# GpSimd takes the clamp of the weights' conversion, and TensorE transposes the identity in its early gaps

## The chip, the cores and the metric

The kernel runs on one core of a Trainium2 chip. The metric is device microseconds (us) of one execution, as the median of several. The core's engines are named as in the profile: PE (TensorE, matrix products and transposes), DVE (VectorE), ACT (ScalarE), POOL (GpSimd) and SP (SyncE, which only issues loads and stores here).

## The reference

What is computed, cut to its core (batch 8, 8 heads, 576 positions, head dimension 64; 4608 tokens, model width 512, inner width 2048):

```python
q_s = np.exp(q - np.max(q, axis=-1, keepdims=True))
q_s = q_s / (np.sum(q_s, axis=-1, keepdims=True) + 1e-09)
k_s = np.exp(k - np.max(k, axis=2, keepdims=True))
k_s = k_s / (np.sum(k_s, axis=2, keepdims=True) + 1e-09)
kv = np.einsum('bhsd,bhse->bhde', k_s, v)
attn = np.einsum('bhsd,bhde->bhse', q_s, kv)        # x: its rows by token, 4608 x 512
r = np.maximum(x @ w_in, 0.0)
out = (s * (r * r) + b) @ w_out
```

Inputs and outputs reach the kernel as float32; the weights arrive in HBM as 64-bit numbers, two 32-bit words each.

## The kernel before

**Work.** Tokens go in 9 blocks of 512 (one for each batch element, 512 of its 576 positions, and a last one of the 64 left over from each). A block has 16 steps, one for each 128 columns of the inner width. Step t makes `h` (12 products of 128x512, line 693), r = relu(h), s r² + b split into a high part `gh` and a low part `gl` (lines 718 to 737), and adds 12 products into the accumulator `acc` (line 760). Every operand is split into two float32r parts, high and low, so three products stand for one. The 144 steps make up nearly all of PE's time.

**Attention.** A head pair u (two heads, four of them in a batch element) gives 128 rows of x. In block 0 and 1 keys and queries are worked on by `k_stream`, `k_pair`, `kv_stream`, `kv_second` and `q_stream`: maxima (L333, L409), subtractions (L411, L474), exponentials on ACT, sums (L417), reciprocals, products (L423), transposes on PE into `kT`, `kn`, `qT`, key-value products `kv` (L295), and `xp` (L437), from which ACT copies x's high part and DVE makes its low part (L446). From block 2 on the work of the next blocks (`k_late`, `q_late`, `kv_late`) goes in between the steps; there GpSimd does the query subtraction (L572) and the query product (L589).

**Weights.** Each of the 16 weight pairs (`st`, 1 MiB of w_in and w_out together) is converted once, in block 0, by `conv_w`. The high word of a number holds sign, exponent and upper mantissa. ACT scales the low word into `low` (L196) and writes the absolute value of the high word into `st`'s low words (L199). DVE puts the sign bits into `low` (L202), clamps the high words, read as floats, to the range that float32's exponents have room for (L207), masks and shifts them (L209), and adds both (L212); ACT rounds the sum to the high part of `w` (L217), and DVE subtracts it for the low part (L219). The first pair is converted in two halves, the others whole (128 x 1024 elements).

**Order.** All instructions stand in an order that is made ahead of time by `Order.run`: every stream of work is a list of `Op`s, each with an engine, a cost in us, a due time and what it needs. The planner takes the engine whose next operation can start first, and there the operation with the smallest due time. Due times are counted in steps: conversions are due `AHEAD` steps ahead of theirs, and the attention of blocks 0 and 1 has hand-set numbers (`DUE_K`, `DUE_Q`, `DUE_V`, `DUE_W`). The planner counts PE at double cost until `COLD` us. Nothing in it ties one engine's costs to what another engine does at the same time. On the chip each engine runs its list in this order, and waits where an input isn't there. Loads are issued by SP in the order of the planner's lists too; `transfers` sets that of the first ones.

```python
first, i = min(can)
eng = heads[i][0].eng
t, i = min(
    ((t, i) for t, i in can if heads[i][0].eng == eng and t <= first + self.NEAR),
    key=lambda c: (heads[c[1]][0].due, c),
)
```

Of the kernel before, what the change touches and what calls it, by code (L numbers as in the profile page):

```python
# [8 lines left out]
F32 = mybir.dt.float32  # L9
# [5 lines left out]
ALU = mybir.AluOpType  # L15
# [11 lines left out]
def attention_moe(ctx: ExitStack, tc: tile.TileContext, q, k, v, w_in, w_out, s, b, out):  # L27
# [10 lines left out]
    TB = NQ * P  # L38
    NTMP = 3
    NFE = 5  # L40
    AHEAD = 1.5
    PACE = 6

    DUE_K = (-30, 0.5, -20, -25, 3.5, 11.5, 12, 19.5)
    DUE_Q = (-18, -32.5, -13.5, -6, 12.5, 9, -30.5, 64.5)
    DUE_V = (-81.5, -28.5, -14, 31)
    DUE_W = -15
    assert DM == H * D and DM == NP * P and 2 * D == P and 2 * LEFT == P and B * LEFT == TB

    const = ctx.enter_context(tc.tile_pool(name="const", bufs=1))  # L50
# [62 lines left out]
    class Order:  # L113
# [1 line left out]


        NEAR, HOP, TRIP, RATE = 0.1, 0.15, 2.8, 0.33
        COLD = 18

        def __init__(self, bufs):  # L120
            self.bufs = bufs
            self.at, self.done, self.pipe = {}, {}, 0.0
            self.taken = {tag: 0 for tag in bufs}
            self.freed = {tag: [] for tag in bufs}

# [16 lines left out]
        def run(self, streams):  # L142
            heads = [[next(g), 0.0, g] for g in streams]
            while heads:
                can = [(self.start(o, ready), i) for i, (o, ready, g) in enumerate(heads)]
                can = [(t, i) for t, i in can if t is not None]
# [4 lines that stand above are left out]
                    key=lambda c: (heads[c[1]][0].due, c),  # L151
                )
                o, ready, g = heads[i]

                heads[i][1] = end = self.at[eng] = t + o.cost * (2 if eng == "PE" and t < self.COLD else 1)
                if o.kb:
                    self.pipe = max(self.pipe, end) + o.kb / 1024 / self.RATE
                    end = self.pipe + self.TRIP
                for tag in o.take:
                    self.taken[tag] += 1  # L160
                for tag in o.free:
                    self.freed[tag].append(end + self.HOP)
                for n in o.gives:
                    self.done[n] = end, "DMA" if o.kb else eng
                heads[i][0] = after = next(g, None)
                if after is None:
                    del heads[i]
                elif not o.kb and (eng != "PE" or after.eng != eng):
                    heads[i][1] = end + self.HOP
# [15 lines left out]
    def conv_w(f, some):  # L185

        due = f - AHEAD if f else DUE_W
        n = some.stop - some.start
        two = n / 2
        last = some.stop == 2  # L190
        yield Op("ACT", 1.04 * two, due, needs=[f"w{f} {i} there" for i in range(some.start, some.stop)], take=["tmp"])
        stg = wst[f][:, some]
        lo, hi = stg[:, :, :, 0], stg[:, :, :, 1]
        low = work.tile([P, n, DO], U32, name=f"low{some.start}_{f}", tag="tmp", bufs=NTMP)

        nc.scalar.activation(low.bitcast(I32), lo, AF.Copy, scale=2.0 ** -29)  # L196
        yield Op("ACT", 1.04 * two, due)

        nc.scalar.activation(lo.bitcast(F32), hi.bitcast(F32), AF.Abs)  # L199
        yield Op("DVE", 0.6 * two, due)  # L200

        nc.vector.tensor_scalar(  # L202
            low.bitcast(U16).rearrange("p n (e t) -> p n e t", t=2)[:, :, :, 1], stg.bitcast(U16)[:, :, :, 3],
            0xC000, None, op0=ALU.bitwise_and
        )
        yield Op("DVE", 0.6 * two, due)
        nc.vector.tensor_scalar(lo.bitcast(F32), lo.bitcast(F32), C_MIN, C_MAX, op0=ALU.max, op1=ALU.min)  # L207
        yield Op("DVE", 0.6 * two, due)
        nc.vector.tensor_scalar(lo, lo, 0x07FFFFFF, 3, op0=ALU.bitwise_and, op1=ALU.logical_shift_left)  # L209
        yield Op("DVE", 1.13 * two, due, free=["w"] if last else (), gives=[f"w{f} {some.stop} read"])  # L210

        nc.vector.tensor_tensor(out=low, in0=lo, in1=low, op=ALU.add)  # L212
        yield Op("ACT", 0.98 * two, due, take=["w"] if some.start == 0 else ())
        if not wt[f]:
            wt[f] = wpool.tile([P, 2, 2, DO], F32R, name=f"w_{f}", tag="w")
        w = wt[f][:, some]
        nc.scalar.copy(w[:, :, 0], low.bitcast(F32))  # L217
        yield Op("DVE", 1.13 * two, due, free=["tmp"], gives=[f"w{f} {i}" for i in range(some.start, some.stop)])
        nc.vector.tensor_tensor(out=w[:, :, 1], in0=low.bitcast(F32), in1=w[:, :, 0].bitcast(F32), op=ALU.subtract)  # L219
        for i in range(n):  # L220
            if some.start + i == 0:
                wi[f] = w[:, i].rearrange("p t (c e) -> p t c e", c=NP)
            else:
                wo[f] = w[:, i]
# [124 lines left out]
    def k_pair(pr):  # L349
        us = (2 * pr, 2 * pr + 1)  # L350
        due = DUE_K[us[0]]

        def sm(n):
            return ps.tile([P, 512], F32, name=f"{n}_{pr}", tag="sm", bufs=1)

        yield Op("DVE", 1.13, due, needs=[f"k{u} there" for u in us])
        kt = by_head(tiles[pr][0])
        kts = [kt[:, 2 * i:2 * i + 2] for i in range(2)]
        m2, m1, km = k_tiles(pr)
        k_max_2(kt, m2)  # L360
        yield Op("DVE", 0.9, due)
        k_max_1(kt, m2, m1)
        yield Op("PE", 0.25, due, take=["sm"])
        kT = sm("kT")
        k_turn(m1, kT)
        yield Op("DVE", 0.35, due, free=["sm"])
        k_top(kT, km)
        yield Op("PE", 0.25, due, take=["sm"])
        mb = spread(km, sm("mb"))
        for i, u in enumerate(us):  # L370
            yield Op("DVE", 0.73, due, free=["sm"] if i else (), gives=[f"k{u} less"])
            k_less(kts[i], mb, i)
        for i, u in enumerate(us):
            yield Op("ACT", 0.63, due, gives=[f"k{u}"])
            k_exp(kts[i])
# [427 lines left out]
    def transfers():  # L803
# [2 lines left out]
        yield from some_k(0, 1)  # L806
        yield from fetch(0)
        yield from some_k(1, 0)
        yield from some_k(1, 1)
        yield from whole(1, 1, "q")  # L810
        yield from whole(0, 2, "v")
        yield from whole(1, 2, "v")
        for f in range(1, NFE):
            yield from fetch(f)
# [39 lines left out]
    def reload_late(pr):  # L854
# [17 lines left out]
        return k_(), q_(), v_()  # L872

    tiles.update({pr: raws[pr % 2 if pr < 2 else 0] for pr in range(NU // 2)})
    order = Order({
        "acc": 2, "big": 1, "sm": 1, "h": 1, "r": 1, "g": 2, "ke": 1, "qf": 1, "qe": 2, "m2": 1, "m1": 1, "top": 1,
        "maxima": 2, "turned": 2, "xleft": 2, "tmp": NTMP, "w": NFC + 1
    })
    E = mybir.EngineType
    late = range(NP, NU // 2)  # L880
    with tc.manual_schedule(engines={E.PE, E.DVE, E.Activation, E.Pool, E.SP}):
# [42 lines left out]
```

## Time and profile before

| | |
|---|---|
| median of 3 runs | 880.31 us (879.52 to 880.44) |
| the profiled execution's own time | 879.32 us |
| its span, first to last instruction | 877.5 us |
| PE busy | 855.6 us (97%) |
| DVE busy | 497.5 us (57%) |
| ACT busy | 356.9 us (41%) |
| POOL busy | 90.9 us (10%) |
| L693 and L760, PE on the chain that ended last | 40% and 41% of the span |

A row of the timeline has the start in us, the length in us, engine, source line, operation, what is written and read, the shapes and a count of merged instructions; in brackets stands the engine's idle time before it and what ended that. On an engine, an instruction's row reaches a little into the next one's, so the pitch from start to start is what a queue of them takes. A row of the groups has busy us and the mean ns of one, then the idle time before it. The windows give each engine's busy us in a stretch. The page's slices show the busy share in tenths, 40 for the span.

### The profile page before, as it was taken

To read this page: it belongs to the slowest core of one execution; us is meant where nothing else is said; L and a number is where in the kernel's file an instruction comes from. 1 tells how busy PE (TensorE), PEld (TensorE's weight loads), DVE (VectorE), ACT (ScalarE), POOL (GpSimd) and SP (SyncE) were. 2 spreads that over 40 slices of the span, in tenths; PEclk is the share of its full clock that TensorE was granted. 3 is DMA by queue.
4 is the path that set the end of the run, shared out by engine and by line. 5 is a ranking of instruction groups with operands and counts; after the bars stand their busy time and mean duration, and the time that the engine had idled before them with its cause. 6 is when DMAs were issued, how large, how long until landed. Compare 5 with 4: busy or idle time off the path is not lost.

```text
span 877.5 us, 11329 instructions
## 1 busy us (share of the span) xinstructions
PE 855.6 (97%) x4360; PEld 705.5 (80%) x4360; DVE 497.5 (57%) x799; ACT 356.9 (41%) x568; POOL 90.9 (10%) x110
## 2 busy tenths in 40 slices
PE   4899999999999999999999999999999999999997
PEld 4677887888888888888888888888888888888886
DVE  7999997566665656564566536663652232232222
ACT  5988854434433333333333333433342322222222
POOL 1000002121121202020112002120200010000000
PEclk9999999999999999999999999999999999999999
DMA  9968034533433414341433243321411000000001
GB/s 246 309 245 269 2 83 119 126 87 86 132 85 110 108 59 109 108 110 36 132 85 85 84 129 88 85 85 70 116 32 52 12 37 1 1 24 25 1 1 48
DMA packets 109957, 79.43 MB, mean 91 GB/s; under 512 B 60624, under 2 KB 103632, under 8 KB 109776
## 3 DMA queue, kind: packets, MB, share of 16 engines
q1 hardware_dynamic: 108496, 77.60, 32.2%
q10 hardware_dynamic: 1408, 1.12, 0.4%
q8 instruction: 34, 0.56, 0.3%
q14 instruction: 19, 0.16, 0.1%
HBM read 60.29 MB, written 18.40 MB: 90 GB/s over the span
## 4 chain that ended last, share of the span: by engine, by line
PE 86%; DVE 6%; DMA 2%; ACT 2%; issue 2%; SPq 1%; ACTq 0%; DVEq 0%
PE acc L760 41%; PE h L693 40%; PE kv L295 2%; PE xp L650 2%; DMA q<-in_q_dram 1%; DMA v<-in_v_dram 1%; DVE low L212 1%; DVE w L219 1%; SPq L284 1%; DVE st L209 1%; DVE low L202 1%; PE xq L650 1%; DVE st L207 0%; ACT st L199 0%; ACT low L196 0%
## 5 line engine op out<-in xcount | busy, mean ns | idle before, releaser
L693 PE MATMUL h<-x,w 128*128 128x512 f32 x1728 | 419.7, 391 | 3.0 <-DVE x L446 1.0
L693 PEld LDWEIGHTS h<-x,w 128*128 128x128 f32 x1728 | 322.6, 188 | 72.4 <-DVE w L219 1.9
L760 PE MATMUL acc<-w,gh 128*128 128x512 f32 x1152 | 357.3, 391 | 0.0
L760 PEld LDWEIGHTS acc<-w,gh 128*128 128x128 f32 x1152 | 214.8, 188 | 45.3 <-ACT o L786 0.4
L731 DVE SCALAR_TENSOR_TENSOR r<-r,sb 128x512 f32<-128x512 f32 x136 | 106.1, 780 | 253.7 <-ACT r L718 253.0
L760 PE MATMUL acc<-w,gl 128*128 128x512 f32 x576 | 224.7, 390 | 0.2 <-DVE gl L735 0.2
L718 ACT ACTIVATE r<-h 128x512 f32<-128x512 f32 x144 | 86.1, 598 | 319.2 <-PE h L693 313.2
L735 DVE SCALAR_TENSOR_TENSOR gl<-r,sb,gh 128x512 fp32r<-128x512 f32 x136 | 106.9, 786 | 60.4 <-ACT gh L733 59.5
L733 ACT ACTIVATE gh<-r,sb 128x512 fp32r<-128x512 f32 x136 | 98.4, 724 | 88.6 <-DVE r L731 88.0
L760 PEld LDWEIGHTS acc<-w,gl 128*128 128x128 f32 x576 | 108.1, 188 | 23.9 <-DVE gl L735 0.9
L572 POOL TENSOR_TENSOR q<-q,qm 128x640 f32<-128x640 f32 x24 | 35.8, 1502 | 133.3 <-DVE qm L570 133.2
L589 POOL TENSOR_TENSOR qe<-qe,qr 128x640 f32<-128x640 f32 x24 | 31.5, 1316 | 32.0 <-DVE qr L585 12.4
L659 DVE TENSOR_TENSOR x<-xp,x 128x512 fp32r<-128x512 f32 (+1 forms) x24 | 13.3, 553 | 20.8 <-ACT x L657 20.3
L576 ACT ACTIVATE qe<-q 128x640 f32<-128x640 f32 x24 | 18.7, 785 | 15.5 <-POOL q L572 15.5
L295 PEld LDWEIGHTS kv<-v,k 128*64 128x64 f32 x600 | 19.8, 143 | 6.0 <-issue 2.8
L635 POOL TENSOR_TENSOR kvhl<-kvf,kvhl 128x256 fp32r<-128x256 f32 x12 | 8.9, 741 | 133.9 <-issue 127.3
L295 PE MATMUL kv<-v,k 128*64 128x65 f32 (+1 forms) x600 | 21.9, 230 | 0.7 <-DMA v<-in_v_dram 0.7
L593 DVE STREAM_TRANSPOSE q<-qe 128x640 f32<-128x640 f32 x24 | 19.6, 818 | 4.5 <-POOL qe L589 4.5
L579 DVE TENSOR_REDUCE qs<-qe 128x20 f32<-128x640 f32 x24 | 19.0, 794 | 5.1 <-ACT qe L576 5.1
L559 ACT ACTIVATE k<-k 128x640 f32<-128x640 f32 x24 | 17.2, 736 | 11.3 <-DVE k L521 11.3
L561 POOL MEMSET k<- 64x128 f32 x24 | 4.8, 200 | 154.5 <-ACT k L559 152.2
L607 DVE TENSOR_TENSOR qT<-qT,qh 128x640 fp32r<-128x640 f32 x24 | 19.7, 821 | 1.7 <-ACT qh L604 1.7
(111 smaller groups left out, 527.9 us busy)
## 6 DMA issues: line engine op xcount, KB each, us to landing
st<-in_moe_w_in_dram SPq DMA_DIRECT2D x16, 512.0 KB, 8.9
st<-in_moe_w_out_dram SPq DMA_DIRECT2D x16, 512.0 KB, 8.9
out_dram<-o SPq DMA_DIRECT2D x16, 512.0 KB, 2.7
turned<-q SPq DMA_DIRECT2D x24, 320.0 KB, 2.4
qT<-turned SPq DMA_DIRECT2D x48, 160.0 KB, 4.3
q<-in_q_dram SPq DMA_DIRECT2D x14, 512.0 KB, 5.3
k<-in_k_dram SPq DMA_DIRECT2D x14, 512.0 KB, 4.3
v<-in_v_dram SPq DMA_DIRECT2D x56, 128.0 KB, 4.9
```

The source lines that it names most:

```text
L295: nc.tensor.matmul(kv[h * D:(h + 1) * D, i], kt[:, i, h, n], vt[:, 2 * i + h, n], start=(n == 0), stop=(n == NT - 1))
L572: nc.gpsimd.tensor_tensor(out=qt, in0=qt, in1=bc(qm, [P, 2, NT, D]), op=ALU.subtract)
L589: nc.gpsimd.tensor_tensor(out=qe_, in0=qe_, in1=qr, op=ALU.mult)
L593: nc.vector.transpose(out=tb, in_=qe.rearrange("p h t n r -> p (h t n r)"))
L607: nc.vector.tensor_tensor(out=ql, in0=qT, in1=qh.bitcast(F32), op=ALU.subtract)
L650: nc.tensor.matmul(t[:, 0:n * D], lhs, rhs[:, a, 0:n], start=(j == 0), stop=(j == len(terms) - 1))
L693: nc.tensor.matmul(hp_, w[:, j, c, :], x[:, c, :], start=(c == 0 and i == 0), stop=(c == NP - 1 and i == 2))
L718: nc.scalar.activation(r, hp_, AF.Relu)
L731: nc.vector.scalar_tensor_tensor(out=r, in0=r, scalar=s_col, in1=r, op0=ALU.mult, op1=ALU.mult)
L733: nc.scalar.activation(gh, r, AF.Identity, bias=b_col)
L735: nc.vector.scalar_tensor_tensor(out=gl, in0=r, scalar=b_col, in1=gh.bitcast(F32), op0=ALU.add, op1=ALU.subtract)
L760: nc.tensor.matmul(acc[blk, j // 2][:, j % 2], g[:, js], w_, start=(f == 0 and i == 0), stop=(f == NFC - 1 and i == 2))
```

## The change

Four things change together.

1. In `conv_w` the clamp of the high words goes from DVE to GpSimd, and the planner counts 1.3 us for it in place of 0.6.
2. `idle` is new: wherever the planner leaves PE without work up to step 0's first product, it puts transposes of the identity into that gap, as many as fill six tenths of it at 0.109 us each, into a PSUM tile that nothing reads (`unused`, in the one buffer that the tiles `h` go through).
3. The planner's numbers are new: `AHEAD`, the due times, `COLD` (18 to 8), two costs of `k_pair`; PE may begin at 3.0.
4. In `transfers`, the keys of u = 3 are loaded after the second pair's queries and the first pair's values.

```diff
-    AHEAD = 1.5
+    AHEAD = 2.5
...
-    DUE_K = (-30, 0.5, -20, -25, 3.5, 11.5, 12, 19.5)
-    DUE_Q = (-18, -32.5, -13.5, -6, 12.5, 9, -30.5, 64.5)
-    DUE_V = (-81.5, -28.5, -14, 31)
-    DUE_W = -15
+    DUE_K = (-5, 1.5, -19.5, -36.5, 4, 19.5, 10, 36.5)
+    DUE_Q = (-12.5, -54, -20, -12, 14, 14.5, -28.5, 69)
+    DUE_V = (-84, -20, -24.5, 39.5)
+    DUE_W = -10
...
-        COLD = 18
+        COLD = 8
...
-            self.at, self.done, self.pipe = {}, {}, 0.0
+            self.at, self.done, self.pipe = {"PE": 3.0}, {}, 0.0
...
+                if eng == "PE":
+                    self.idle(t - self.at[eng], "h" in o.take)
...
-        yield Op("DVE", 0.6 * two, due)
-        nc.vector.tensor_scalar(lo.bitcast(F32), lo.bitcast(F32), C_MIN, C_MAX, op0=ALU.max, op1=ALU.min)
+        yield Op("POOL", 1.3 * two, due)
+        nc.gpsimd.tensor_scalar(lo.bitcast(F32), lo.bitcast(F32), C_MIN, C_MAX, op0=ALU.max, op1=ALU.min)
...
-        yield Op("DVE", 1.13, due, needs=[f"k{u} there" for u in us])
+        yield Op("DVE", 0.69, due, needs=[f"k{u} there" for u in us])
...
-        yield Op("DVE", 0.9, due)
+        yield Op("DVE", 0.85, due)
...
-        yield from some_k(1, 1)
         yield from whole(1, 1, "q")
         yield from whole(0, 2, "v")
+        yield from some_k(1, 1)
         yield from whole(1, 2, "v")
...
+    unused = [ps.tile([P, 512], F32, name="unused", tag="h")]
+
+    def idle(us, last):
+        if last:
+            unused.clear()
+        for _ in range(int(0.6 * us / 0.109) if unused else 0):
+            nc.tensor.transpose(unused[0][:, 0:P], ident, ident)
```

Source lines move by 3 from `conv_w` on: L202, L207, L209, L212, L217 and L219 of before are L205, L210, L212, L215, L220 and L222 after. The orders below show three places, on the engines of which the prediction speaks.

PE's list from its beginning, in the program after the change (`kT`, `kn` and `qT` are transposes of keys, of their exponentials and of queries):

```order
L884 MATMUL unused<-ident 128x128 x24
L333 MATMUL kT_153<-ident,k_91 128x128 x5
L884 MATMUL unused<-ident 128x128 x10
L346 MATMUL kn_191<-ident,ke_175 128x128 x4
L347 MATMUL kn_191<-ident,ke_175 64x128
L333 MATMUL kT_204<-ident,k_91 128x128 x5
L884 MATMUL unused<-ident 128x128 x2
L430 MATMUL qT_220<-ident,qe_161 128x128 x5
L884 MATMUL unused<-ident 128x128 x10
```

The rows of L884 are new; the others stand in the order they had. In all 58 such transposes are put in up to step 0.

GpSimd's list after the change, from the memset that ends the preparation (`st` are the weights as loaded, the first pair in two halves):

```order
L837 MEMSET one 128x1
L210 TENSOR_SCALAR st_117<-st_117 128x512 x2
L284 MEMSET v_93 64x4x64
L285 MEMSET v_93 128x20
L210 TENSOR_SCALAR st_226<-st_226 128x1024
L210 TENSOR_SCALAR st_239<-st_239 128x1024
L210 TENSOR_SCALAR st_304<-st_304 128x1024
L210 TENSOR_SCALAR st_315<-st_315 128x1024
L210 TENSOR_SCALAR st_436<-st_436 128x1024
L210 TENSOR_SCALAR st_492<-st_492 128x1024
L485 MEMSET k_91 64x2x64 x2
L210 TENSOR_SCALAR st_527<-st_527 128x1024
```

Before, this list had only the memsets here. The two halves and the 15 whole clamps are now in one queue with the memsets of v and k.

DVE's list before the change, up to the lower part of the weights of step 13 (`w_1039`; their words are `low_13`, and `low_14` belongs to step 14):

```order
L207 TENSOR_SCALAR st_806<-st_806 128x1024
L455 TENSOR_TENSOR m_3_1004<-k_91 128x512
L209 TENSOR_SCALAR st_806<-st_806 128x1024
L458 TENSOR_TENSOR m_3_1005<-m_3_1004 128x256
L459 TENSOR_TENSOR m_3_1005<-m_3_1004,k_91 64x256
L212 ISA low_13_919<-st_806,low_13_919 128x2048
L202 TENSOR_SCALAR low_14_978<-st_839 128x1024
L409 TENSOR_REDUCE qm_1044<-q_92 128x10
L219 TENSOR_TENSOR w_1039<-low_13_919,w_1039 128x2x512
```

And the same place after the change, up to `w_1143`, the weights of step 13 there:

```order
L477 TENSOR_TENSOR k_91<-k_91,mb_1065 128x640
L215 ISA low_13_1019<-st_866,low_13_1019 128x2048
L205 TENSOR_SCALAR low_14_1074<-st_929 128x1024
L205 TENSOR_SCALAR low_15_1084<-st_987 128x1024
L420 TENSOR_REDUCE qs_1124<-qe_806 128x10
L412 TENSOR_REDUCE qm_1130<-q_92 128x10
L212 TENSOR_SCALAR st_929<-st_929 128x1024
L731 TENSOR_TENSOR gl_1101<-r_1099,gh_1100 128x512
L215 ISA low_14_1074<-st_929,low_14_1074 128x2048
L734 SCALAR_TENSOR_TENSOR r_1168<-r_1168,sb 128x512
L222 TENSOR_TENSOR w_1143<-low_13_1019,w_1143 128x2x512
```

The clamp is gone from the list, and the conversions of steps 14 and 15 and work on queries and keys have come ahead of step 13's last operation.

More of the change, by code (lines that the diff above doesn't have):

```diff
@@ L117, in attention_moe, with __init__ @@
         NEAR, HOP, TRIP, RATE = 0.1, 0.15, 2.8, 0.33
-        COLD = 18
-        def __init__(self, bufs):
-            self.bufs = bufs
-            self.at, self.done, self.pipe = {}, {}, 0.0
+        COLD = 8
+        def __init__(self, bufs, idle):
+            self.bufs, self.idle = bufs, idle
+            self.at, self.done, self.pipe = {"PE": 3.0}, {}, 0.0
             self.taken = {tag: 0 for tag in bufs}
@@ L877, in attention_moe @@
         "maxima": 2, "turned": 2, "xleft": 2, "tmp": NTMP, "w": NFC + 1
-    })
+    }, idle)
     E = mybir.EngineType
```

## The prediction

> **What bounds the kernel now.** I read the page's slices and its chain first, then the windows, then the timelines of VectorE (DVE) and TensorE (PE) side by side. Times are us from the start of the span.
>
> ```profile
> PE   4899999999999999999999999999999999999997
> ...
> DVE  7999997566665656564566536663652232232222
> ...
> PE 86%; DVE 6%; DMA 2%; ACT 2%; issue 2%; SPq 1%; ACTq 0%; DVEq 0%
> ```
>
> One digit is 22 us. From the third slice on PE is full, and a full PE can't be sped up by this change; what can be won or lost lies in the first 130 us, where DVE stands at 9 as well.
>
> ```profile
> 6.00:40.00 34.00, 24.28 (x171) 19.19 (x172) 31.92 (x61) 26.25 (x48) 0.45 (x2) 1.00 1.05 301
> 40.00:130.00 90.00, 88.78 (x463) 71.36 (x462) 89.05 (x131) 73.95 (x97) 1.50 (x4) 1.00 0.48 153
> ```
>
> The busy columns are PE, weight loads, DVE, ACT, POOL. In the 90 us after the start PE is busy for 88.78 and DVE for 89.05: both are full at once. Which one leads is seen where a step's weights are made just before PE wants them. Counting the rows of L219 and of L693, step 13 is this:
>
> ```profile
> 106.75 1.23 DVE L219 TENSOR_TENSOR w<-low,w 128x1024 fp32r<-128x1024 f32 x1 [0.22 <-ACT w L217]
> 107.89 0.68 DVE L728 TENSOR_TENSOR gl<-r,gh 128x512 fp32r<-128x512 f32 x1
> ...
> 111.15 2.98 PE L693 MATMUL h<-x,w 128*128 128x512 f32 x12
> ```
>
> The weights of step 13 are done at 107.9, and PE starts on them at 111.15: 3.3 us of margin, and nothing to spare elsewhere. DVE decides block 0 as soon as it gets more work.
>
> **Part 1: the clamp leaves DVE.** Two DVE instructions of each form in a row give the pitch of one:
>
> ```profile
> 88.80 1.42 DVE L202 TENSOR_SCALAR low<-st 128x1024 uint16<-128x1024 uint16 x2
> 90.08 1.24 DVE L219 TENSOR_TENSOR w<-low,w 128x1024 fp32r<-128x1024 f32 x1
> 91.21 1.32 DVE L207 TENSOR_SCALAR st<-st 128x1024 f32<-128x1024 f32 x2
> 92.41 1.32 DVE L209 TENSOR_SCALAR st<-st 128x1024 uint32<-128x1024 uint32 x2
> 93.62 2.37 DVE L212 CUSTOM_DVE_ANT_0 low<-st,low 128x2048 uint16<-128x2048 uint16 x2
> 95.89 0.71 DVE L728 TENSOR_TENSOR gl<-r,gh 128x512 fp32r<-128x512 f32 x1
> ```
>
> L207 goes: (92.41 - 91.21) / 2 = 0.60 us, and about 0.33 for each of the two halves of the first weights. L202 is 0.64, L219 1.13, L212 1.14, L209 0.60.
>
> **Part 2: DVE's sum up to the weights of step 13.** I count the instructions ahead of that L219 in the two orders. After has 13 clamps and 2 halves less, 13 x 0.60 + 2 x 0.33 = -8.5 us. But the new due times pull other work ahead of it: two each of the query maxima (L409), query subtractions (L411), query sums (L417) and key subtractions (L474), one query product (L423), each 0.73 by the pitch of the rows below; one L202, L209 and L212 more (2.4); and small ones that leave +1.3 (eps and reciprocal 0.3, a key maximum 0.3, an L728 and an L731 1.3, less one L446, 0.6).
>
> ```profile
> 6.33 1.54 DVE L409 TENSOR_REDUCE qm<-q 128x10 f32<-128x640 f32 x2 [6.33 <-DMA q<-in_q_dram]
> 7.80 1.55 DVE L411 TENSOR_TENSOR q<-q,qm 128x640 f32<-128x640 f32 x2
> ...
> 23.27 0.76 DVE L333 TENSOR_REDUCE km<-kT 128x1 f32<-128x576 f32 x1 [0.96 <-PE kT L330]
> ...
> 25.15 0.69 DVE L446 TENSOR_TENSOR x<-xp,x 128x512 fp32r<-128x512 f32 x1 [0.40 <-ACT xleft L237]
> ...
> 49.68 1.23 DVE L219 TENSOR_TENSOR w<-low,w 128x1024 fp32r<-128x1024 f32 x1 [0.43 <-ACT w L217]
> ```
>
> 9 x 0.73 + 2.4 + 1.3 = +10.3, so +1.8 net. DVE's idle in brackets, here and in the row at 106.75, is 0.96 + 0.40 + 0.43 + 0.22 = 2.0; I give the change all of it, since PE's part of the start gets quicker (part 4). Without any new cost the weights of step 13 would be ready at 107.9 + 1.8 - 2.0 = 107.7. Ahead of step 13 PE has done one more group of key-value products than before, (125.50 - 124.18) = 1.3 us by these rows:
>
> ```profile
> 124.18 1.39 PE L295 MATMUL kv<-v,k 128*64 128x65 f32 x40
> 125.50 0.77 PE L427 MATMUL qT<-ident,qe 128*128 128x128 f32 x5
> ```
>
> At equal work, before stands at 111.15 + 1.3 = 112.45. So the change is worth 107.7 - 112.45 = **-4.8 us**, if GpSimd's work is free for DVE. PE could be there still earlier (its starting gaps shrink with DVE's work ahead of step 1, and so do its waits), so DVE is what binds.
>
> **Part 3: what GpSimd's clamp costs DVE.** No trace shows a GpSimd TENSOR_SCALAR of this size. But the later blocks show what a GpSimd operation that reads SBUF does to a DVE operation with two SBUF operands:
>
> ```profile
> 184.97 1.27 POOL L589 TENSOR_TENSOR qe<-qe,qr 128x640 f32<-128x640 f32 x1 [1.46 <-PE h L693]
> ...
> 185.15 1.64 DVE L731 SCALAR_TENSOR_TENSOR r<-r,sb 128x512 f32<-128x512 f32 x1 [0.39 <-ACT r L718]
> ...
> 190.59 0.75 DVE L731 SCALAR_TENSOR_TENSOR r<-r,sb 128x512 f32<-128x512 f32 x1 [2.25 <-ACT r L718]
> ```
>
> The same L731 takes 0.75 alone and 1.64 when issued 0.18 after GpSimd began. It lost 0.89, so GpSimd held it off for 0.89 + 0.18 = 1.07 of its 1.27 us. The other way round:
>
> ```profile
> 181.63 0.75 DVE L735 SCALAR_TENSOR_TENSOR gl<-r,sb,gh 128x512 fp32r<-128x512 f32 x1
> 181.78 1.74 POOL L589 TENSOR_TENSOR qe<-qe,qr 128x640 f32<-128x640 f32 x1 [4.65 <-PE acc L760]
> 182.30 0.81 DVE L579 TENSOR_REDUCE qs<-qe 128x20 f32<-128x640 f32 x1
> ```
>
> GpSimd waited 0.47 (1.74 - 1.27) for the L735 ahead of it, and the reduction L579 ran beside it at its usual length. So they take turns, whole instruction by whole instruction, and reductions don't take part. [...]
>
> How long is GpSimd's clamp on 1024 elements? The rows around it:
>
> ```profile
> 1.04 0.31 POOL L91 MEMSET k<- 64x256 f32 x1
> ...
> 116.30 0.20 POOL L482 MEMSET k<- 64x128 f32 x1 [49.73 <-ACT k L481]
> ...
> 699.32 1.35 POOL L679 TENSOR_TENSOR x<-xleft_all,x 128x512 fp32r<-128x512 f32 x1 [46.94 <-ACT x L677]
> ```
>
> Writing alone grows by 0.11 us per 128 elements, which makes 0.31 + 6 x 0.11 = 0.97 for 1024: the short end. Two full inputs take 1.35 for 512, 2.7 for 1024: the long end. I take 1.27, the L589 row (one full input, the other broadcast), with its 1.07 of holding; the planner's own cost is 1.3, and its 1.28 for L589 fits that row. Holding is then 0.77 at the short end (0.97 less the 0.2 that L589 doesn't hold) and 2.5 at the long one.
>
> What share of it hits DVE? Between 40 and 130 the operations with at most one SBUF input are these; the columns ahead of the mean are busy us:
>
> ```profile
> L474 DVE TENSOR_TENSOR k<-k,mb 128x640 f32<-128x640 f32 x4 | 3.2, 806 | 0.0
> L409 DVE TENSOR_REDUCE qm<-q 128x10 f32<-128x640 f32 x3 | 2.4, 809 | 0.0
> L417 DVE TENSOR_REDUCE qs<-qe 128x10 f32<-128x640 f32 x3 | 2.4, 809 | 0.0
> L446 DVE TENSOR_TENSOR x<-xp,x 128x512 fp32r<-128x512 f32 x2 | 1.4, 692 | 0.0
> ```
>
> With the small ones about 11 of 89 us, so 88% is exposed; in the start, where a maximum or a sum stands at every turn, I estimate 60%. If GpSimd can't get in between, DVE soon meets L209 (now L212), which waits for the clamp, and then stands still for the whole of it; so it pays either way. Behind that L212 the low words (L215), w's lower part (L222) and the gl of the steps are queued, and PE waits for those. On GpSimd's own queue the clamps stand among the memsets of k, which wait for ACT's exponentials; DVE's key subtractions come earlier than before, so I cost that at nothing. Up to step 13 that is 11 x 0.88 x 1.07 + 3 x 0.60 x 1.07 + 2 halves x 0.3 = 10.4 + 1.9 + 0.6 = **12.9 us**, for 8.5 us that were taken off.
>
> **Part 4: the transposes of the identity.** Five transposes of a kind:
>
> ```profile
> 6.95 1.30 PE L330 MATMUL kT<-ident,k 128*128 128x128 f32 x5 [6.95 <-DMA k<-in_k_dram]
> ...
> 21.95 1.27 PE L330 MATMUL kT<-ident,raw 128*128 128x128 f32 x5
> ...
> 24.22 0.71 PE L427 MATMUL qT<-ident,qe 128*128 128x128 f32 x5
> ```
>
> Up to 22 us PE runs at half speed, though the granted clock reads 1.00, and from 24.2 at full. The 58 added transposes fill gaps: the first 24, at (1.30 / 5) = 0.26 at most, last from about 2.0, when the identity is there, to 8.2 at the latest; the key maximum that needs the transposes behind them isn't started on DVE before 9.26 in before (two L411 of 0.73 from 7.80), which hides all but 0.2 of it. Then the groups up to 24 us take about 0.55 us less each. DVE is full there, so this buys only the idle of part 2 (0.96 and 0.40), which is counted already. [...]
>
> **Part 5: the loads.** The keys of the fourth head pair (u = 3) and the queries q2 go behind other loads on SP's queue.
>
> ```profile
> 17.54 7.90 DMA q<-in_q_dram
> ...
> 28.12 0.81 DVE L409 TENSOR_REDUCE qm<-q 128x10 f32<-128x640 f32 x1
> ```
>
> q2 landed at 25.4 and was used at 28.1. One weight of 1 MiB more ahead of it costs 1.05 MB at 301 GB/s (the window from 6 to 40), 3.5 us, so 28.9; its L409 now stands behind the whole of the first weights' conversion, at about 30 us by the sum of the rows ahead of it. If that cover is gone, DVE waits 1 us at most. I cost it at nothing.
>
> **Sum.** -4.8 + 12.9 = +8.1 us. Against the profiled execution's own 879.3 us (span 877.5) that is 887.4; the median of the runs shown, 880.3, lies 1.0 above that execution, so the two readings are 887.4 and 888.4. Steps 14 and 15 have up to 1.2 us of PE's waits in before, of which some go: I say **887**.
>
> **Rivals.**
> - *GpSimd costs DVE little* (0.3 us each or less, because most clamps fall into DVE's waits or under reductions). For it: the start has many reductions. Against it: 88% of the rows between 40 and 130. 15 clamps' worth x 0 to 0.3 = 0 to 4.5: 879.3 - 4.8 = 874.5, up to 879. It decides below 4.8 / 15 = 0.32 us per clamp. Chance 0.27.
> - *The two cancel*: holding at the short end, 0.77, and half of it hidden, 0.4 to 0.5 us each: +1.2 to +2.7, 880.5 to 882. Chance 0.13.
> - *The clamp is long*: holding 1.6, between 1.07 and the long end's 2.5, gives 14 x 0.88 x 1.6 = 20, +15, 894; the long end itself 31, 905. Chance 0.10.
> - *The transposes don't raise the clock.* Then DVE keeps its 0.96 and 0.40 of idle, +1.4 on any of these: 888.4 on the forecast. One in five, within the others.
> - The forecast, loss per clamp 0.55 to 1.07: 883 to 891. Chance 0.50.
>
> **Range and chances.** 0.2% (1.8 us) is about what a measurement of this kernel can tell from no change. Faster than 878.5 is the first rival, 0.27 with nearly all its width; within, most of the second, 0.10; slower the rest, 0.63. The range 875.5 to 893 leaves out the long clamp (0.10) and the best fifth of the first rival (0.06). Cases of both signs carry weight: the forecast's own range is 883 to 891.
>
> **What would show it.** Right: GpSimd's clamps near 1.3 us; DVE's conversion operations (after's L205, L212, L215, L222) with means above their 0.7 to 1.2; DVE full to 130 and later; PE with waits for w and gl between 45 and 130. Wrong: those DVE means unchanged, DVE below 9 tenths before 120 us, and PE without gaps after 40. Transposes of five at 0.7 by 13 us would show part 4 right, 1.3 wrong. What would break the forecast most simply is a clamp that holds DVE off for under a third of a microsecond.

## The result, and the profile after

| | us, median | range | runs |
|---|---|---|---|
| before | 880.31 | 879.52 to 880.63 | 5 |
| after | 899.72 | 898.07 to 900.18 | 5 |

The ratio is 1.0223, 95% interval 1.0211 to 1.0235: 19.4 us slower. The forecast had the sign (887, +8) and less than half of the size, and the time lies outside its range. The profiled execution took 898.07 us (span 896.3).

The slices of the page after (PE, DVE, POOL; 22.4 us each) and its chain:

```profile
PE   7788989999999999999999999999999999999997
...
DVE  7998986565656653766365646564653233223222
POOL 3556742021202200211020202020200011000000
...
PE 84%; DVE 6%; issue 3%; POOL 2%; ACT 2%; DMA 1%; SPq 1%; ACTq 0%; POOLq 0%; DVEq 0%
```

PE used to be full from the third slice on; now it has gaps up to the sixth, and POOL, which had nothing on the chain, holds 2% of it. The windows after say where (busy us of PE, weight loads, DVE, ACT, POOL, then the granted clock):

```profile
6.00:40.00 34.00, 24.51 (x206) 19.71 (x205) 32.67 (x56) 25.57 (x47) 14.47 (x7) 0.93 1.05 286
40.00:130.00 90.00, 79.27 (x395) 60.92 (x394) 84.24 (x103) 65.91 (x83) 56.95 (x17) 0.97 0.50 163
```

From 40 to 130 PE is busy 79.27 us instead of 88.78, and DVE, for which the change was to make room, 84.24 instead of 89.05. Both stand still for longer than before, so what ends their waits lies elsewhere. POOL went from 1.50 to 56.95. The group of its clamps, over the whole span:

```profile
L210 POOL TENSOR_SCALAR st<-st 128x1024 f32<-128x1024 f32 (+1 forms) x17 | 69.3, 4090 | 34.9 <-ACT st L202 34.7
```

One clamp takes 4.09 us in the mean (two of the 17 are halves), not 1.27. The stretch from 70 to 85 us shows what follows from this; POOL first, then DVE, then PE, from the timelines after:

```profile
72.06 11.25 POOL L210 TENSOR_SCALAR st<-st 128x1024 f32<-128x1024 f32 x3
```

```profile
72.56 1.34 DVE L414 TENSOR_TENSOR q<-q,qm 128x640 f32<-128x640 f32 x1
...
75.91 1.56 DVE L212 TENSOR_SCALAR st<-st 128x1024 uint32<-128x1024 uint32 x1 [1.54 <-POOL st L210]
...
77.72 1.21 DVE L215 CUSTOM_DVE_ANT_0 low<-st,low 128x2048 uint16<-128x2048 uint16 x1
79.61 1.56 DVE L212 TENSOR_SCALAR st<-st 128x1024 uint32<-128x1024 uint32 x1 [0.68 <-POOL st L210]
81.09 0.68 DVE L731 TENSOR_TENSOR gl<-r,gh 128x512 fp32r<-128x512 f32 x1
```

```profile
77.61 0.61 PE L763 MATMUL acc<-w,gh 128*128 128x512 f32 x2
81.83 0.50 PE L763 MATMUL acc<-w,gl 128*128 128x512 f32 x1 [3.60 <-DVE gl L731]
...
85.06 3.69 PE L696 MATMUL h<-x,w 128*128 128x512 f32 x12
```

Three clamps of 3.75 us in a row. A mask (L212) waits for the first one's result (1.54 us), and is then held off at its own start, because the second clamp has just begun (1.56 instead of 0.69). The next mask waits for the second clamp's result (0.68), and is held by the third. Behind it in DVE's queue stands the gl of the step (L731), an operation that has nothing to do with the weights' conversion; PE waits 3.60 us for it. And when PE goes on, the 12 products of the next step take 3.69 us instead of 2.88:

```profile
84.00:86.00 2.00, 2.00 (x6) 1.52 (x6) 2.00 (x4) 1.92 (x3) 0.00 (x0) 0.50 1.03 359
```

The granted clock (the number after POOL's) is 0.50 there. Over the whole start, DVE's own waits for the clamp, and PE's longest waits, are these (sum in us, times, longest one):

```profile
DVE st L212 <- POOL st L210: 6.3, 5, 2.6
```

```profile
PE acc L763 <- DVE gl L731: 5.4, 4, 3.6
PE h L696 <- DVE x L449: 3.6, 3, 2.6
...
PE kv L298 <- POOL k L485: 1.4, 1, 1.4
```

### The profile page after: what moved, and what is told of

Same layout as the page of the kernel before. It is cut to its first block, busy times and chain, and to the rows that moved or that the text cites. A ratio compares the mean times of both kernels' runs of the same rounds, so it can differ in the third digit from the quotient of the medians.

```text
span 896.3 us, 11467 instructions
## 1 busy us (share of the span) xinstructions
PE 866.1 (97%) x4418; PEld 711.7 (79%) x4418; DVE 503.3 (56%) x782; ACT 355.9 (40%) x568; POOL 157.9 (18%) x127
## 4 chain that ended last, share of the span: by engine, by line
PE 84%; DVE 6%; issue 3%; POOL 2%; ACT 2%; DMA 1%; SPq 1%; ACTq 0%; POOLq 0%; DVEq 0%
PE acc L763 40%; PE h L696 40%; PE kv L298 2%; POOL st L210 2%; PE xp L653 2%; DVE w L222 1%; DVE low L215 1%; DVE st L212 1%; DMA k<-in_k_dram 1%; DVE low L205 1%; PE xq L653 1%; DMA q<-in_q_dram 1%; DVE gl L731 0%; ACT w L220 0%; PE xp L440 0%
## 5 line engine op out<-in xcount | busy, mean ns | idle before, releaser
L734 DVE SCALAR_TENSOR_TENSOR r<-r,sb 128x512 f32<-128x512 f32 x136 | 108.0, 794 | 252.0 <-ACT r L721 251.3
L210 POOL TENSOR_SCALAR st<-st 128x1024 f32<-128x1024 f32 (+1 forms) x17 | 69.3, 4090 | 34.9 <-ACT st L202 34.7
L220 ACT CAST w<-low 128x1024 fp32r<-128x1024 f32 (+1 forms) x17 | 16.9, 997 | 11.1 <-DVE low L215 11.0
```

Of the source, the lines that this page charges most:

```text
L210: nc.gpsimd.tensor_scalar(lo.bitcast(F32), lo.bitcast(F32), C_MIN, C_MAX, op0=ALU.max, op1=ALU.min)
L734: nc.vector.scalar_tensor_tensor(out=r, in0=r, scalar=s_col, in1=r, op0=ALU.mult, op1=ALU.mult)
```

## The experiments

The line numbers of a kernel differ by a few where lines were added. Differences are to the kernel before as it was timed beside each run (879.67 to 880.31). In round brackets stands the ratio to it, with its 95% interval.

**First, parts of the change with the plan made anew.** The obvious first step: put the clamp back, leave it out, or make one part alone, and let the planner order everything for that. Theories: T1, the clamp's length and the holds on DVE make the loss; T2, the new due times do.

clamp_dve, the change with the clamp back on DVE:

```diff
-        yield Op("POOL", 1.3 * two, due)
-        nc.gpsimd.tensor_scalar(lo.bitcast(F32), lo.bitcast(F32), C_MIN, C_MAX, op0=ALU.max, op1=ALU.min)
+        yield Op("DVE", 0.6 * two, due)
+        nc.vector.tensor_scalar(lo.bitcast(F32), lo.bitcast(F32), C_MIN, C_MAX, op0=ALU.max, op1=ALU.min)
```

> The kernel after the change with one edit: the clamp is done by DVE again, and the planner counts 0.6 us for it there. Theory 1 (the clamp on GpSimd costs all of the loss: its rows last 4.1 us in the mean, DVE is held off or waits for it): 874 to 881 us, PE without waits for w and gl between 45 and 130. Theory 2 (the new due times or the transposes cost it, the clamp little): above 890 us.

Measured 887.61 (1.0091 [1.0076, 1.0106]), +7.9: between both theories.

only_clamp, the same edit the other way round in the kernel before (no transposes, old due times):

> The kernel before with one edit: the clamp goes to GpSimd with the planner's 1.3 us, old due times, no transposes. Theory 1: 893 to 903 us, near the whole change. Theory 2: 878 to 884 us.

Measured 908.69 (1.033 [1.0315, 1.0346]), +29: worse than the whole change.

clamp_out, the change without the two lines of the clamp (exponents aren't held):

> The kernel after the change without any clamp, on no engine, so it leaves out the clamp of the high words. It is the case in which the clamp is free for DVE, which the prediction put at -4.8 us: 874 to 876 us if that term is right. Theory 2: above 885 us.

Measured 890.39 (1.0128 [1.0112, 1.0143]), +10.7: slower with no clamp at all than with DVE's, which its expectation counts as theory 2.

transposes_only, the kernel before with `idle`, `COLD` 8 and PE's start at 3.0:

> The kernel before with the transposes of the identity alone (and PE's start at 3.0 and COLD 8 in the planner), clamp on DVE, old due times. Theory 1: 877 to 881 us, since DVE is full in the start and the groups on PE get shorter by half without moving it; first products of step 1 at 37 to 39.4. Theory 2, in the form that the transposes cost it: above 885 us.

Measured 883.9 (1.0053 [1.0036, 1.007]), +4.2: between both theories.

What follows: less about the clamp than about the method. A planner that is given one other cost makes another order, and an order that its due times weren't fitted to costs up to 10 us by itself (clamp_out against kept_out below: the same instructions). These four can't tell the theories apart.

**Second, the order kept.** The planner keeps its entry for the clamp, so all other instructions stand where the change has them, and only what is issued at that entry differs.

kept_out:

```diff
         yield Op("POOL", 1.3 * two, due)
-        nc.gpsimd.tensor_scalar(lo.bitcast(F32), lo.bitcast(F32), C_MIN, C_MAX, op0=ALU.max, op1=ALU.min)
```

In this and the later expectations, "the port" is the author's word for whatever lets GpSimd hold DVE off; the runs show the hold, not what makes it.

> The order of the changed kernel on every engine, word for word, with only the clamp instruction left out (what is left out: exponents aren't held to float32's range, which these inputs don't reach often or at all). In clamp_out and clamp_dve the planner was given other costs, and so put block 1's start in another order; here it is not. T1 (the clamp instruction costs it all: port and waits for its result): the predicted -4.8 us without any new cost, 872 to 878. T2 (the new due times and loads cost several us of their own, whoever clamps): 885 or more. In between: both have a share.

Measured 880.62 (878.59 to 883.2; 1.001 [0.9998, 1.0022]), +0.7. In between: the order and the transposes without any clamp neither cost several us nor gain the 4.8. Step 13 of kept_out on DVE and on PE (its line numbers are one less than after's):

```profile
107.69 2.37 DVE L221 TENSOR_TENSOR w<-low,w 128x1024 fp32r<-128x1024 f32 x2
```

```profile
37.24 3.02 PE L695 MATMUL h<-x,w 128*128 128x512 f32 x12 [0.97 <-ACT r L720]
...
46.94 0.50 PE L762 MATMUL acc<-w,gl 128*128 128x512 f32 x1 [0.23 <-DVE gl L730]
...
109.49 2.88 PE L695 MATMUL h<-x,w 128*128 128x512 f32 x12
```

The first of the two L221 is step 13's: done at 108.9, where the prediction had 107.7. Of the 1.2 us between them, 1.06 are waits of DVE that are still there (0.17, 0.19, 0.49 and 0.22 us, all before 36 us), where the prediction gave the change all 2.0 of before's. PE starts the step at 109.49 and, after 37.24, has waited for 0.23 us and once more for 0.10. It is late because it is full. That is 3.0 ahead of the 112.45 that the prediction has as before's equal work, not 4.8. Then these 3.0 are lost at the start of block 1, kept_out first, then before:

```profile
134.02 0.71 PE L429 MATMUL qT<-ident,qe 128*128 128x128 f32 x5
135.46 1.24 PE L439 MATMUL xp<-qf,kvf 128*128 128x256 f32 x4 [0.73 <-ACT qf L432]
137.37 0.50 PE L695 MATMUL h<-x,w 128*128 128x512 f32 x1 [0.68 <-ACT x L445]
138.21 1.22 PE L695 MATMUL h<-x,w 128*128 128x512 f32 x2 [0.34 <-DVE x L448]
140.12 5.24 PE L695 MATMUL h<-x,w 128*128 128x512 f32 x12 [0.69 <-ACT r L720]
```

```profile
132.61 0.71 PE L427 MATMUL qT<-ident,qe 128*128 128x128 f32 x5
133.52 2.35 PE L693 MATMUL h<-x,w 128*128 128x512 f32 x9 [0.20 <-ACT r L718]
135.70 1.14 PE L437 MATMUL xp<-qf,kvf 128*128 128x256 f32 x4
136.43 0.87 PE L760 MATMUL acc<-w,gh 128*128 128x512 f32 x2
```

The chain qT, qf, xp, x, h goes from PE to ACT and DVE and back. In before, the nine first products of block 1's step 0 and the accumulations of step 15 stand between its links. In the new order they have been spent by then, and PE waits at each link: 0.73 + 0.68 + 0.34 + 0.69 = 2.4 us, instead of 0.20. In this execution the granted clock also fell, to 0.53 from 138 to 140 and 0.50 from 140 to 144: the 12 products take 5.24 instead of 2.88, and the two ahead of them 1.22 instead of 0.73, 2.8 in all. -3.0 + 2.2 + 2.8 = +2.0; the span is 879.7 against 877.5.

kept_dve, the same place in the plan, but `nc.vector` in place of `nc.gpsimd`:

> The order of the changed kernel kept, the clamp at the same place of the plan but issued on VectorE, 0.60 us each. T1: 8.5 us of VectorE's time come back up to step 13 on top of kept_out, 879 to 885, and 15 to 20 us below the changed kernel. T2: 888 to 894.

Measured 887.53 (1.0087 [1.0066, 1.0108]), +7.6. Just below T2's range: 6.9 over kept_out for a DVE clamp that was to cost 8.5, and 12 below the change.

kept_side:

```diff
-        nc.gpsimd.tensor_scalar(lo.bitcast(F32), lo.bitcast(F32), C_MIN, C_MAX, op0=ALU.max, op1=ALU.min)
+        nc.gpsimd.tensor_scalar(hi.bitcast(F32), hi.bitcast(F32), C_MIN, C_MAX, op0=ALU.max, op1=ALU.min)
```

> The order kept; GpSimd clamps the high words in place, which nobody reads again, instead of their absolute values (so the clamp of the exponents is left out, and the same length of GpSimd work stands at the same place). [...] If the port alone makes the loss (theory P, the prediction's part 3 with its 12.9 us): within 3 us of the changed kernel, 896 to 901. If the wait for a result that comes after some 4 us makes as much (theory W: 6.3 us of waits at L212, and PE's clock that falls in the gaps): 884 to 892. Near kept_out: the port costs nothing.

Measured 891.93 (1.0137 [1.0122, 1.0152]), +12.0: theory W, at its upper edge. 11.3 us over kept_out come from GpSimd's work that nobody needs, and 7.4 more from waiting for it. Its clamps have to follow the signs (L205), which read the words that they overwrite; the first one starts at 13.79 us instead of 12.13. The 11.3 include 2.4 us of PE waiting for a memset of k that stands behind a clamp on POOL's queue:

```profile
118.99 0.34 PE L298 MATMUL kv<-v,k 128*64 128x65 f32 x4 [2.43 <-POOL k L485]
```

The group of the masks from 24 to 130 us in kept_out, kept_side and after (busy us, mean ns, then idle):

```profile
L211 DVE TENSOR_SCALAR st<-st 128x1024 uint32<-128x1024 uint32 (+1 forms) x16 | 10.7, 667 | 0.0
```

```profile
L212 DVE TENSOR_SCALAR st<-st 128x1024 uint32<-128x1024 uint32 (+1 forms) x16 | 13.4, 834 | 0.0
```

```profile
L212 DVE TENSOR_SCALAR st<-st 128x1024 uint32<-128x1024 uint32 (+1 forms) x16 | 16.0, 1001 | 6.3 <-POOL st L210 6.3
```

The one group shows both costs: longer by holds in the second, longer again and waiting 6.3 us in the third. Other rows are held as well. Added up row by row over the same list, as far as 130 us, DVE's rows are 11.6 us longer in kept_side than in kept_out, and 13.5 us longer in the change; in wait_long below, which has no clamp of that length, 0.4.

The rows of the change also show at what point a clamp holds DVE. A mask, a sign operation or one with two inputs in SBUF that is held just behind the start of a clamp gets to run some 2.8 us before the clamp's end, so after the first 0.95 us of its 3.75: the mask at 75.91 ends at 77.47 and takes 0.69 by itself, the clamp ends at 79.58. So are held two signs at 56.09 (2.32 us for both; 1.41 at 70.43), and of those with two inputs L731 at 93.11 (1.60 for 0.68) and L215 at 98.76 (2.10 for 1.21). Two signs that came within 0.06 us of the start of a clamp's row (28.70 and 87.07, 0.76 each) ran at their usual length, and the clamp's row is the longer one (5.97 us at 87.01). Two-input operations that come later run at their usual length, up to the end (L222 at 82.83 takes 1.21 us across the end of the third clamp, at 83.3). A mask at 59.42 (1.55 for 0.69) and a sign at 101.45 (1.63 for 0.78), in the last microsecond of their clamps, are held as well, nearly up to the clamp's end; the mask's rows:

```profile
56.26 4.16 POOL L210 TENSOR_SCALAR st<-st 128x1024 f32<-128x1024 f32 x1 [0.43 <-ACT st L202]
59.42 1.55 DVE L212 TENSOR_SCALAR st<-st 128x1024 uint32<-128x1024 uint32 x1
```

kept_nofill, the change with `range(0)` in `idle`, so without its 58 transposes:

> The changed kernel without the 58 transposes of the identity; order otherwise kept. If they buy VectorE's waits of 0.96 and 0.40 us at the start, as part 4 has it: 900 to 902. If other waits hide them: 899 to 900. If they hurt (PE's work that has to wait behind them): below 898.5.

Measured 898.43 (897.74 to 901.71; 1.0217 [1.0195, 1.0239]), +18.5 where the change has +19.4. That is at the bound where they would hurt, but the two intervals overlap: the transposes do nothing here that these runs can tell.

**Third, the clamp's length and its wait.**

forms, clamp_dve with 18 clamps of spent words by GpSimd in later blocks:

```diff
+            yield Op("POOL", 4.0, 0, needs=[f"h{36 + 3 * i}"])
+            st = wst[NFC - 1].bitcast(F32)
+            a = (st[:, :, :, 0], st[:, 0].rearrange("p e t -> p (e t)"), st[:, 0, :, 0])[i % 3]
+            if i % 2:
+                nc.gpsimd.tensor_scalar(a, a, C_MIN, None, op0=ALU.max)
+            else:
+                nc.gpsimd.tensor_scalar(a, a, C_MIN, C_MAX, op0=ALU.max, op1=ALU.min)
```

> clamp_dve with 18 clamps of spent words by GpSimd in blocks 2 and later, where VectorE stands at 5 to 6 tenths: every third over 1024 elements at a stride of two words, over 1024 side by side, over 512 at a stride of two words, each in turn with both limits and with one. If the stride makes the clamp long, the 1024 side by side take 1.0 to 1.4 us and the strided 3.75; if the two limits do, those with one limit take about half; if VectorE's turns make it long, the shortest of each form are near 1.3; if the length is the elements' alone, 1024 take 3.7 and 512 take 1.9 in every form.

Its own time (890.72, one run) says nothing here. From POOL's timeline, L808 having two limits and L806 one, in order of time: i = 0 (two limits, at a stride), i = 4 (two, side by side), i = 13 (one, side by side), i = 14 (two, 512 elements), i = 15 (one, at a stride):

```profile
259.20 3.76 POOL L808 TENSOR_SCALAR st<-st 128x1024 f32<-128x1024 f32 x1
...
329.66 3.63 POOL L808 TENSOR_SCALAR st<-st 128x1024 f32<-128x1024 f32 x1
...
495.55 2.77 POOL L806 TENSOR_SCALAR st<-st 128x1024 f32<-128x1024 f32 x1
508.40 1.99 POOL L808 TENSOR_SCALAR st<-st 128x512 f32<-128x512 f32 x1
510.47 2.88 POOL L806 TENSOR_SCALAR st<-st 128x1024 f32<-128x1024 f32 x1
```

The length is the operation's own, by elements and limits: 3.63 us for 1024 elements side by side, 3.76 at the stride of two words, 1.99 for 512. One limit alone takes 2.77 and 2.88. These are the usual lengths of their forms; some of the 18 took up to 0.5 longer. Neither of the two layouts, nor an emptier DVE, brings it near 1.3.

wait_alone, in the change's order:

```diff
-        nc.gpsimd.tensor_scalar(lo.bitcast(F32), lo.bitcast(F32), C_MIN, C_MAX, op0=ALU.max, op1=ALU.min)
+        for i in range(14 * n):
+            nc.gpsimd.memset(spare[i % 2], 0.0)
+        nc.gpsimd.tensor_scalar(lo[:, :, 0:1].bitcast(F32), lo[:, :, 0:1].bitcast(F32), C_MIN, C_MAX, op0=ALU.max, op1=ALU.min)
```

> The order kept; in place of GpSimd's clamp stand 28 memsets of 4 columns of a spare tile (14 for a half) and a clamp of the first column alone, so that VectorE's mask waits for GpSimd about as long, while GpSimd reads next to nothing (the clamp of the other columns is left out). If the loss of 7.5 us between kept_side and the changed kernel is the wait for a late result, and needs no hold on VectorE: 880.6 + 5 to 8 = 886 to 889. If it comes from the clamp's work on the same tile as VectorE's: 880 to 883. If small writes hold VectorE off like the clamp: above 892.

Measured 883.55 (1.0047 [1.003, 1.0065]), +3.9, which is 3.2 over kept_out: between. GpSimd's 28 memsets took 2.2 to 2.9 us here, though, less than a clamp. So it was made longer in wait_long (42 memsets):

> wait_alone with 42 memsets instead of 28 per conversion, about 3.3 + 0.5 us, near the clamp's own 3.75 to 4; the clamp of all but the first column is left out. wait_alone's GpSimd work was 2.4 to 2.9 us and cost 2.9 us over kept_out. If the price is the wait for a late result: 886 to 889. If lateness costs little without the hold on the port (VectorE would be quick enough to catch up): 882 to 884.5, and the 7.5 us between kept_side and the changed kernel are the two together.

Measured 888.43 (1.0088 [1.0071, 1.0105]), +8.3: 7.6 over kept_out, against the 7.4 between kept_side and the change. Its POOL rows and its masks (here L215, from the groups of 24 to 130 us):

```profile
68.55 3.35 POOL L212 MEMSET spare<- 128x4 f32 x42
71.90 0.22 POOL L213 TENSOR_SCALAR st<-st 128x2 f32<-128x2 f32 x1
```

```profile
L215 DVE TENSOR_SCALAR st<-st 128x1024 uint32<-128x1024 uint32 (+1 forms) x16 | 11.0, 690 | 5.9 <-POOL spare L212 3.5 <-POOL st L213 2.4
```

The mask runs at its own 0.69 us, so nothing holds DVE, and waits 5.9 us for a result that is about as late as a clamp's. The wait has its price by itself, and 1 us less of lateness takes more than half of it away.

told, the change with `Op("POOL", 4.0 * two, due)`:

> The changed kernel with the planner told 4.0 us for the clamp instead of 1.3, so that it puts other work of VectorE between a clamp and the mask that waits for it. If the wait for the result is a matter of the order: the 7.5 us go, and some of the port's loss with them, 889 to 893. If the port and VectorE's fullness set the time whatever the order: 897 to 901.

Measured 899.2 (1.0225 [1.0209, 1.0241]), +19.5, the second case: the right length in the plan, with these due times, doesn't help. In told, no wait of DVE for L210 is left among those listed, and PE waits 3.3 us for w, 2.9 for the memset of k and 7.5 for gl and gh:

```profile
PE h L696 <- DVE w L222: 3.3, 3, 1.5
PE kv L298 <- POOL k L485: 2.9, 1, 2.9
PE acc L763 <- ACT gh L736: 2.8, 1, 2.8
PE acc L763 <- DVE gl L731: 2.6, 1, 2.6
PE acc L763 <- DVE gl L738: 2.1, 2, 1.4
```

The waits stand at other places now; the time is the same. Due times fitted to a clamp of 4 us were not tried.

before_pool, the kernel before with `nc.gpsimd` at the clamp and its entry `Op("DVE", 0.6 * two, due)` kept, so in the old order:

> The order of the kernel before on every engine, with the clamp issued on GpSimd at its old place, just ahead of VectorE's mask. The mask then waits for nearly the whole clamp. If a clamp costs its 3.75 us in a full VectorE, less the 0.60 taken off, and the margin of 3.3 us at step 13 takes some: 15 x 3.2 - 3 = 45, above 915. If VectorE can do other work in the wait (it can't, its order is fixed) 893 to 900. only_clamp, where the planner knew 1.3, took 908.7: between.

Measured 892.04 (1.0134 [1.0117, 1.0151]), +12.4, just below the lowest of what was expected. So GpSimd's clamp costs 12.4 us more than DVE's in the old order, and 19.4 - 7.6 = 11.8 more in the new one.

**Fourth, what there was to gain.**

before_out, the kernel before with the clamp's instruction left out and its entry kept (exponents aren't held):

> The order of the kernel before on every engine, with the clamp left out (exponents aren't held): the most that any way of taking the clamp off VectorE could buy in the old order. If VectorE binds block 0, as the prediction has it: 8 us or so less up to step 13, 871 to 873. If TensorE is itself full there (its waits from 40 to 130 us sum to 1.2 us in the kernel before, and the first step could start some 2 us earlier): 876 to 878.5. If nothing hangs on it: 879 to 880.

Measured 877.64 (0.9971 [0.9959, 0.9983]), -2.5: the middle case. Nothing else moved, and DVE has 15 clamps and 2 halves less. The window of 40 to 130 us:

```profile
40.00:130.00 90.00, 89.62 (x473) 73.45 (x471) 84.97 (x122) 72.86 (x97) 1.16 (x4) 1.00 0.51 159
```

PE goes from 88.78 to 89.62 of 90 and has nothing more to give; DVE now has 5 us of idle that nothing uses. In this order no way of taking the clamp off DVE, were it free, can bring more than 2.5 us.

before_fill, the kernel before with `idle` and its transposes, `COLD` and PE's start as they were:

> The kernel before with the transposes of the identity in TensorE's gaps and its order otherwise kept (transposes_only had a new plan too, and took 883.9). If they raise the clock early and VectorE's 0.96 and 0.40 us of waiting at the start go: 878 to 879.3. If not, or if other waits hide it: 879.5 to 880.5.

Measured 879.1 (877.84 to 881.17, 10 runs; 0.9988 [0.9979, 0.9998]), -1.0: the first case. It is the only kernel with the whole computation that comes out ahead of before and after, and barely: its interval only just leaves out no change.

## Why the prediction had the sign and not the size

The sum of the steps, as differences to the kernel before:

| step | predicted | measured | from |
|---|---|---|---|
| order, due times, transposes, no clamp on DVE | -4.8 | +0.7 | kept_out |
| GpSimd's clamp holds DVE off | +12.9 | +11.3 | kept_side less kept_out; its DVE rows are 11.6 longer |
| its result is late | 0 | +7.4 | change less kept_side; 7.6 by wait_long |
| sum | +8.1 | +19.4 | |

The split between the last two is that of kept_side, in which no mask waits for a clamp. In the change itself DVE's rows are 13.5 us longer, and its masks wait 6.3 us.

- **Part 1, -8.5 us for the clamp off DVE**: the DVE time is right (0.60 us a clamp), its worth wasn't. In the new order the clamp on DVE costs 6.9 (kept_dve), in the old one 2.5 (before_out).
- **Part 2, the first step that failed.** "PE could be there still earlier (...), so DVE is what binds." The ledger itself was 1.2 us off (108.9 for 107.7), mostly by waits of DVE that it took for gone. But once DVE is relieved, PE is full from 37 us on, and gains only what its first steps gain: 3.0, not 4.8. And the sum stopped at step 13. What the new order does later, at the start of block 1, was covered only by "some" of 1.2 us of waits going; kept_out has 2.4 us of new waits there, and the clock's fall behind them. The change has the same four gaps, of 0.73, 0.68, 0.34 and 0.69 us. The view that would have shown it was at hand: the new order of PE around the first x of block 1.
- **Part 3, the hold: right in kind, and in size by luck.** A held mask takes 1.56 instead of 0.69, so 0.87 where 1.07 was taken, and the sum came to 11.3 for 12.9. Masks and signs, for which the prediction had no run, are held too. The 0.88 in its sum counts them in, and no run shows that share; what the runs show in its place is a mean of the masks of 834 ns in kept_side for 667 in kept_out, and of the signs of 819 for 766. But the clamp is not 1.27 us with 1.07 of holding, it is 3.75 with about 0.9 at a time: the length was three times too short, and the share of it that holds nearly four times too large, so that the two errors nearly cancel. "So they take turns, whole instruction by whole instruction" is wrong: at 77.72 the addition L215, with two operands in SBUF, runs at its usual 1.21 us in the middle of a clamp (75.83 to 79.58), and L731 at 81.09 at its 0.68 in the middle of the next. Had a clamp held for the whole of its length, those two would have been held, and 15 clamps could have cost up to 15 x 3.75 = 56 us, an estimate from the length of the row; the rows show the hold for parts of it only.
- **Part 3, the length, the second step that failed.** The range of 0.97 to 2.7 us had both ends wrong: a memset and a product of two inputs were taken as bounds of a TENSOR_SCALAR with two limits, which is 3.63 to 3.76 (forms). The rival "the clamp is long", with a chance of 0.10, priced more length as more holding (894 to 905). The measured time lies in that range, but by another way: the holding stayed, and the result's lateness came on top. The text saw the place ("DVE soon meets L209 (now L212), which waits for the clamp") but booked it as an alternative to the hold, not on top of it. "On GpSimd's own queue ... I cost that at nothing" fell with it: PE waits 1.4 us for a memset of k behind a clamp.
- **Part 4, the transposes: half right.** That PE would be fast with its gaps filled was the author's estimate; before has no filled gap that shows it. Transposes of five at 6.9 us take 0.74 after (0.83 in before_fill, in the old order), for 1.30 before, as said. But behind a gap of 2.06 us on PE, and four more that take 0.66 at 10.80, they are slow again, 1.09 at 11.41 and 1.30 at 12.71, which the prediction had named as a sign of being wrong (the granted clock reads 0.77 from 10 to 13 us and 0.67 from 13 to 16); from 16.35 on they stay fast, where before gets there at 24.22. They buy nothing beside the clamp, 1.0 in the old order:

```profile
12.71 1.30 PE L430 MATMUL qT<-ident,qe 128*128 128x128 f32 x5
...
16.35 0.71 PE L333 MATMUL kT<-ident,raw 128*128 128x128 f32 x5
```

- **Part 5, loads at nothing**: in kept_out DVE waits 0.49 us for q2 at 30.36, within the 1 us that the prediction allowed and part of the 1.06 above. The loads weren't tried by themselves.
- **Rivals.** That GpSimd costs little or cancels (0.40 together) is refuted by kept_side.

What stays open is why GpSimd holds DVE at those parts of its instruction and not at others.

## What to carry to other kernels

The operation that changed its engine cost three things here: what it holds up on the engine that it left (DVE's rows 11.6 us longer in kept_side), its own length on the new one (3.75 us for 0.60), and the lateness of its result for the queue that waits behind the consumer (7.4 us). Price all three, and the last from the length of that very operation; where no row has it, neighbours of another kind are no bounds: 0.97 to 2.7 us by them, 3.63 to 3.76 measured. Before an engine is relieved, ask how full the next one is: here, in the old order, TensorE had 2.5 us to give, whatever VectorE was spared. And where a planner sets the order, an experiment keeps the planner's entries and changes only what is issued; otherwise it measures another order.

## What the runs showed of the hardware that was not expected

- In forms, GpSimd's clamp of float32 takes 3.5 ns per element of a partition with two limits (3.63 us / 1024) and 2.7 with one (2.77 / 1024); the stride of two words adds less than 5% (3.76 and 2.88 us). In the rows of the change it holds VectorE's masks, signs and two-input operations off in the first 0.95 us of its 3.75 (the mask at 75.91, 1.56 for 0.69), in its last microsecond only masks and signs (1.55 at 59.42, 1.63 at 101.45; L222 at 82.83 keeps its 1.21), and in between none of them (a mask at 72.42 in kept_side 0.69, a sign at 34.59 in the change 0.75, L215 at 77.72 1.21).
- Behind the same small gaps PE went on at a granted clock of 0.50 in one run and of 1.00 in another. After the gaps of 0.73, 0.68 and 0.34 us, kept_out went on at a granted clock of 0.50 for some 7 us (0.53, 0.50, 0.50 and 0.77 in the four windows of 2 us from 138 on; 12 products in 5.24 us). The change has the same gaps in the same order, and its clock did not fall (1.00 from 152 to 166 us):

```profile
154.72 1.24 PE L440 MATMUL xp<-qf,kvf 128*128 128x256 f32 x4 [0.73 <-ACT qf L433]
156.63 0.50 PE L696 MATMUL h<-x,w 128*128 128x512 f32 x1 [0.68 <-ACT x L446]
157.47 0.73 PE L696 MATMUL h<-x,w 128*128 128x512 f32 x2 [0.34 <-DVE x L449]
158.88 3.03 PE L696 MATMUL h<-x,w 128*128 128x512 f32 x12 [0.69 <-ACT r L721]
```

  That may be why the order with gaps has the wider spread (kept_out 878.59 to 883.2 in 10 runs, the kernel before beside it 877.93 to 880.83 in 13); it was not shown run by run. What decides it, no run here shows.
